# Scores-times-v as pairs of 64-row matmuls, in long one-mode stretches: a fused attention and mixer kernel

## The chip, the cores and the metric

The kernel runs on one core of a Trainium2 chip. The time is the device time of one execution in microseconds (us); where several executions are given, their median and their range are named. "The profile" is the record of one execution: a page of summaries, and a trace that can be asked for groups of instructions, waits, the chain of work that ended last, and a timeline. PE is TensorE's matmuls and PEld its weight loads, DVE is VectorE, ACT is ScalarE, POOL is GpSimd, SP is the engine that issues most transfers.

## The reference, cut to what matters

Eight batches of a gated attention without softmax, followed by an MLP mixer over tokens and then over channels:

```
B, S, D = 8, 3008, 256;  d_qk = 64;  d_tok = 256;  d_ch = 1536
scores = (z @ z.T) / S                      # S x S, symmetric
attn   = max(scores, 0) ** 2
x      = u * (attn @ v)                     # gate
h      = max(x.T @ w_tok1, 0) @ w_tok2      # over tokens
y      = x + h.T
out    = y + max(y @ w_ch1, 0) @ w_ch2      # over channels
```

All matmuls take bf16 operands and accumulate in float32.

## The kernel before, in words

**Tiles.** A batch has NQ = 6 query blocks of 512 columns (the last has 448) and NG = 6 key groups of GK = 4 tiles of 128 keys; the 24th tile of keys has 64 rows. Everything is held transposed: channels on partitions, tokens along the free axis.

**Attention, step by step.** `score_run` (L386) makes scores: one unit is two 64-row matmuls (d_qk = 64, one on the upper and one on the lower half of the array, L405) that write the two banks of one PSUM tile `sc`. `relu` evacuates a unit on ACT (L443; L431 for blocks on the diagonal) into half of an `at` tile in SBUF, and `square` squares it on DVE (L451, L479). As scores are symmetric, from batch 1 on only blocks with g >= q are computed and the others are made by a transposing DMA (`flip`, L498; `flip_tiles`, L491). `av_matmul` (L526, matmul at L539) multiplies with v: per query block, two accumulators `acc0` and `acc1` (dh = 0, 1, the two halves of the 256 channels), 23 matmuls of 128 rows each, and one of 64 rows for the last tile of keys; these two (`do_tails`, L561) run as a pair on the two halves of the array. `gate` (L622, L634) multiplies an accumulator with u on DVE into `xT`; a transposing DMA on SP makes the tile that the mixer reads.

**Mixer, in pieces.** When a batch's attention is done, `add_mixer` (L665) lists its work as pieces: 6 of `tok1` (L681, 8 matmuls of 256 columns each), 6 of `tok2` (L698), and, block by block, six of `ch1` (L742, 4 matmuls of 512 columns, evacuated as `h2pre` on ACT at L755 or on DVE at L757) and four of `ch2` (L784, 12 matmuls of 256 columns; a residual add on DVE at L797 and a store). So the mixer of batch b runs beside the attention of batch b + 1, and the mixer of batch 7 runs alone at the end.

**PSUM.** It has eight banks. `acc0` and `acc1` have one each; the other six are three two-bank tiles with the tag `ps`, taken in turn by scores, mixer pieces and early transposes (`RING = 3`, L297; `take_slot`, L661).

**What orders the work.** The program's order is computed when it is built: the loop at L1037 keeps a clock for every engine, knows what each piece costs (`column_time`, L337; a change between 64-row and 128-row matmuls costs 0.095 in `on_pe`, L343), and picks at each step among "scores", "av" (four matmuls of one accumulator, `do_half`, L586) and "mixer". A budget keeps the mixer's progress in step with the attention's, which makes the three kinds alternate piece by piece. ACT's and DVE's instructions are written in the order in which this plan starts them (`push`, L303; `run_engines`, L321). The chip then runs each engine's list in that order, with semaphores between engines.

The functions that the diff touches, with what calls them:

Of the kernel before, what the change touches and what calls it, by code (L numbers as in the profile page):

```python
# [13 lines left out]
P = 128  # L14
# [41 lines left out]
def kernel(  # L56
# [118 lines left out]
    def fill(n, tag="ps", bufs=3):  # L175

        wp = psum.tile([P, QW], F32, tag=tag, name="wp", bufs=bufs)
        for _ in range(n):
            nc.tensor.matmul(
                wp[:], zero[:, :P], zero[:], start=True, stop=True, skip_group_check=True)  # L180
# [117 lines left out]
    ring = [Done(0.0) for _ in range(RING)]  # L298
# [87 lines left out]
    def score_run(us, start):  # L386
        slots = sorted((d for d in ring if d.t is not None), key=lambda d: d.t)
        for unit in us:
            (b, q, g), pr = unit
            zT = zTs[b].rearrange("p t s -> p (t s)")  # L390
            W = widths[q]
            slot = slots.pop(0)
            ring.remove(slot)
            begin = max(start, slot.t, known(turned[b, q], turned[b, g]))
            cost = column_time(W)
            if triangle(b, q, g):

                cost = (column_time(QW), column_time(P))[pr]
            begin, start = on_pe(begin, "half", cost)
            sc = psum.tile([P, 2, QW], F32, tag="ps", name="sc", bufs=3)  # L400
            for r, i, c0, c1 in parts(unit):
                k = z_tile(b, r, g * GK + i) * P
                m = z_tile(b, r, q * GK) * P
                h = slice(r * d_qk, (r + 1) * d_qk)
                nc.tensor.matmul(  # L405
                    sc[:, r, c0:c1], zT[h, k:k + P], zT[h, m + c0:m + c1],
                    start=True, stop=True)
            if pr == 0:
                live["at"] += 1
                at_free.remove(min(at_free))  # L410
            busy = 0.92
            if triangle(b, q, g):
                busy = (0.87, 0.43)[pr]
            if grain(b, q, g) < GK and pr == 0:
                early[b, q, g] = [Done() for _ in range(GK)]
            done = push("act", begin + cost + 0.21, busy, busy + 0.16,
                        lambda t, unit=unit, sc=sc: relu(unit, sc, t))
            ring.append(done)
# [93 lines left out]
    class Block:  # L512
        def __init__(self, b, q):
            self.b, self.q, self.W = b, q, widths[q]
            self.todo = key_order(b, q)[1]
            self.slot = 0
            self.g = None
            self.steps, self.half = [], 0
            self.acc = [None] * DT
            self.tails = False  # L520
            self.parts = {}
# [4 lines left out]
    def av_matmul(blk, g, i, dh, stop):  # L526
        first = blk.acc[dh] is None
        if first:
            blk.acc[dh] = psum.tile([P, QW], F32, tag=f"acc{dh}", name=f"acc{dh}", bufs=1)
        rows = slice(0, P)  # L530
        if g * GK + i == KT - 1:
            rows = slice(dh * TAIL, (dh + 1) * TAIL)
        rhs = blocks[blk.b, blk.q, g][1][rows, i]
        o = blk.acc[dh][:, :blk.W]
        if len(rhs.shape) == 3:
            o = o.rearrange("p (j s) -> p j s", s=P)
        else:
            rhs = rhs[:, :blk.W]
        nc.tensor.matmul(  # L539
            o, vs[blk.b, g][rows, i, dh * P:(dh + 1) * P], rhs, start=first, stop=stop,  # L540
            skip_group_check=True)
# [9 lines left out]
    def block_ready(blk, g):  # L551
        e = blocks.get((blk.b, blk.q, g))
        return FAR if e is None else known(e[0])

# [6 lines left out]
    def do_tails(blk, start):  # L561
        on_pe(start, "half", column_time(blk.W))
        blk.parts.setdefault(LAST, 2)
        for dh in range(DT):
            av_matmul(blk, LAST, GK - 1, dh, False)
        blk.tails = True
        finished(blk, LAST)

    def next_half(t):

        blk = cur[0]
        if blk is None:
            return FAR, None
        if blk.g is not None:
            dh, tiles = blk.steps[blk.half]
            events = early.get((blk.b, blk.q, blk.g), [])[tiles[0]:tiles[-1] + 1]
            return max(t, known(acc_free[dh], *events)), blk.g
        at = max(t, known(acc_free[0]))
        ready = [(block_ready(blk, g), i) for i, g in enumerate(blk.todo)]
        soon = [i for r, i in ready if r <= at + 0.05]  # L580
        if soon:
            return at, blk.todo[soon[0]]
        r, i = min(ready)
        return max(at, r), blk.todo[i]

    def do_half(start, g):  # L586
# [17 lines left out]
        for i in tiles:  # L604
            av_matmul(blk, g, i, dh, final and i == tiles[-1])
        if final:
            acc_free[dh] = push(
                "dve", end + 0.21, 0.61, 0.75, lambda t, dh=dh: gate(blk, dh, t), first=1,
                room=("xT", "x") if dh == 0 else lambda: (blk.b, blk.q) in xTs)
        blk.half += 1  # L610
        if blk.half == len(blk.steps):
            blk.g = None
            finished(blk, g)
            if final:
                if blk.q == NQ - 1:
                    add_mixer(blk.b)
                m = blk.b * NQ + blk.q + 1
                cur[0] = Block(m // NQ, m % NQ) if m < B * NQ else None
# [3 lines left out]
    def gate(blk, dh, t):  # L622
        b, q, W = blk.b, blk.q, blk.W
        acc = blk.acc[dh]
# [36 lines left out]
    def take_slot():  # L661
        slot = min((d for d in ring if d.t is not None), key=lambda d: d.t)
        ring.remove(slot)

    def add_mixer(b):  # L665
# [6 lines left out]
        def tok1(q, end):  # L672
            if q == 0:
                take_slot()
                st["a_ps"] = psum.tile([P, DT, d_tok], F32, tag="ps", name="a_ps", bufs=3)
# [9 lines left out]
            if q == NQ - 1:  # L685
                def evacuate(t):
                    st["a"] = sb.tile([P, 2, D], BF16, tag="a", name="a_sb", bufs=1)
                    nc.scalar.activation(st["a"][:], st["a_ps"][:], ACT.Relu)
                    a_done.t = t
                ring.append(push("act", end + 0.21, 0.5, 0.65, evacuate, first=1))  # L690

        def tok2(q, end):
            take_slot()
            W = widths[q]
            h = psum.tile([P, DT, QW], F32, tag="ps", name="h_ps", bufs=3)
# [21 lines left out]
            ring.append(push("dve", end + 0.21, 1.12, 1.25, add))  # L717
# [12 lines left out]
        def ch1(q, c2, end):  # L730
            take_slot()
# [6 lines left out]
            hp = psum.tile([P, 2, QW], F32, tag="ps", name="hp", bufs=3)  # L738
# [12 lines left out]
            def evacuate(t):  # L751
# [6 lines left out]
                if q == NQ - 1:  # L758
                    if c2 == 0 and b % 2 == 0:
# [5 lines left out]
            ring.append(push(engine, end + 0.21, busy, busy + 0.16, evacuate,  # L765
                             done=h2_done[q, c2]))
# [3 lines left out]
        def ch2(q, half, i, end):  # L770
            apart = alone(q, half)
            if i == 0 or apart:
                take_slot()
                st["op"] = psum.tile([P, 2, D], F32, tag="ps", name="op", bufs=3)
# [18 lines left out]
            def residual(t):  # L793
# [25 lines left out]
                if over:  # L819
                    live["us"] -= 1  # L820
            ring.append(push("dve", max(end + 0.21, known(st["turned", q])), 0.62, 0.75,
                             residual))
# [44 lines left out]
    def next_piece(t):  # L867

        best = FAR, None
        slots = [d.t for d in ring if d.t is not None]  # L870
# [87 lines left out]
    def late_z(c, landed):  # L958
# [4 lines left out]
        def turn(end):  # L963
            take_slot()
            zp = psum.tile([P, GK, P], F32, tag="ps", name="zp", bufs=3)
            turn_on_pe(zr[0], zp)
            turned[0, c] = Done()
            ring.append(push(
                "dve", end + 0.2, 0.66, 0.8,
                lambda t: nc.vector.tensor_copy(zTs[0][:, c * GK:c * GK + GK, :], zp[:]),  # L970
                first=1, done=turned[0, c]))
# [5 lines left out]
    def first_u(landed):  # L977
# [3 lines left out]
        def turn(end):  # L981
            take_slot()
            up = psum.tile([P, QW // P * DT, P], F32, tag="ps", name="up", bufs=3)
# [5 lines left out]
            ring.append(push("dve", end + 0.2, 1.15, 1.3, lambda t: evacuate(up)))  # L989

        def evacuate(up):
            uTs[0, 0] = sb.tile([P, QW // P, DT, P], BF16, tag="uT", name="uT", bufs=3)
            nc.vector.tensor_copy(
                uTs[0, 0].rearrange("p t h s -> p (t h) s"), up[:])
# [19 lines left out]
    flat = NQ * NG * 1.73 + NQ * (NQ + 1) / 2 * 0.63  # L1014
    fill(7)

    for c in range(DT):
        zp = psum.tile([P, GK, P], F32, tag=f"acc{c}", name=f"zp{c}", bufs=1)
        turn_on_pe(double_first_z(c), zp)
        nc.scalar.copy(zTs[0][:, c * GK:c * GK + GK, :], zp[:])  # L1020
    for c in range(DT, GK):
        turn_first_z(c)
    fill(1)
# [12 lines left out]
    STARVED = 0.7  # L1036
    while cur[0] is not None or heads or tails:  # L1037
# [10 lines left out]
        n = can_score(done_units, RING)  # L1048
        slots = sorted(d.t for d in ring if d.t is not None)
        n_now = min(n, len(slots))  # L1050
        ts = FAR
        if n_now:
            at = max(t, has_turned(units[done_units:done_units + n_now]))
            ts = max([at] + [slots[i] - 0.1 - 0.216 * i for i in range(n_now)])
# [13 lines left out]

        pick = None

        together = (
            blk is not None and blk.q > 1 and blk.b < B - 1 and not blk.tails
            and blk.slot == 0 and t + 0.3 < tails_ready(blk) < FAR)
        if n_now and not together and ts <= t + NOW and (whole or (low and n_now >= 2)):
# [10 lines left out]
        elif budget > 0 and tm <= t + NOW:  # L1085
            pick = "mixer"
        elif ta <= t + NOW:
            pick = "av"
        elif tm <= t + NOW and (budget > -5.0 or blk is None):
            pick = "mixer"  # L1090
        else:
            options = [(ta, "av"), (tm, "mixer")]
            if n_now and (whole or low):
# [7 lines left out]
            if blk is not None and blk.b == 0 and blk.q == 0 and blk.acc[1] is None:  # L1101
                idle = int((when - t) / 0.22)
                if idle:
                    fill(idle, "acc1", 1)
            pick = what

        if pick == "scores":
            if blk is not None and tails_ready(blk) <= t + 0.3:
# [46 lines left out]
```

## Time and profile before

| what | value |
|---|---|
| median of 3 executions | 1183.68 us |
| the three executions | 1168.08, 1183.68, 1184.21 us |
| profiled execution, span from first to last instruction | 1166.2 us |
| nearest executed time to that span | 1168.08 us, 1.9 us more |
| busy: PE, DVE, ACT, POOL | 1152.4, 554.7, 509.0, 129.0 us |
| matmuls and weight loads of the program, each | 7057 |
| first weight load of batch 1's scores-times-v | at 91.84 us |
| last scores-times-v matmuls | up to 1071 us |
| last matmul starts | 1161.6 us |

The page gives no time of its own for the profiled execution besides the span. A row of the groups names the line, the engine, the operation, output and input tiles, shapes and count; then the total busy time and the mean of one in ns, and how long that engine had stood idle before these instructions, with what ended the idleness. Durations of matmuls include their way through the array, and successive ones overlap, so what a matmul costs is the distance between successive starts. A line of the timeline merges neighbours of one kind: its start, how long the group lasted up to the end of its last member, and the count. A few matmul records are missing in the trace, so counts in merged lines can be short; weight loads are complete.

### The profile page before, as it was taken

Reading aid. Unit: us, or ns where it says so; the run is one execution under the profiler, and the core shown is the slowest. Engines: PE = TensorE matmul, PEld = TensorE weight load, DVE = VectorE, ACT = ScalarE, POOL = GpSimd, SP = SyncE. Lnnn points to the kernel's source line nnn. Section 1 sums busy time; section 2 is a strip of 40 time slices with the busy share of each in tenths; the row PEclk is TensorE's granted clock in tenths of the full one; section 3 lists DMA queues with packets and bytes.
Section 4 is the critical chain, followed back from the end, with each engine's and each line's share of the span. In section 5 each row is a group of like instructions: output and inputs, shape, how many; then the busy total and the mean of one; then the engine's idle time right before and its main releaser. Section 6 shows DMA issues by size and latency. Waiting matters only on the chain.

```text
span 1166.2 us, 17678 instructions
## 1 busy us (share of the span) xinstructions
PE 1152.4 (99%) x6964; PEld 629.8 (54%) x7057; DVE 554.7 (48%) x842; ACT 509.0 (44%) x636; POOL 129.0 (11%) x281
## 2 busy tenths in 40 slices
PE   9999999999999999999999999999999999999998
PEld 3334554655546555565555645566454655555666
DVE  6666541556434563435424365243752546512544
ACT  7886552436332453344623355343442444513221
POOL 4510110102001020010300102001020001000000
PEclk9999999999999999999999999999999999999999
DMA  8999596987969789895979859686897968442121
GB/s 161 185 178 193 125 159 135 163 152 137 168 127 172 148 144 164 116 184 126 117 178 160 174 119 174 153 162 115 169 158 138 176 132 169 92 101 55 50 82 64
DMA packets 472500, 165.54 MB, mean 142 GB/s; under 512 B 436256, under 2 KB 450144, under 8 KB 472416
## 3 DMA queue, kind: packets, MB, share of 16 engines
q1 hardware_dynamic: 444560, 131.70, 57.2%
q0 software_dynamic: 27344, 32.32, 20.9%
q8 instruction: 55, 0.90, 0.3%
q10 hardware_dynamic: 512, 0.38, 0.1%
q14 instruction: 29, 0.24, 0.1%
HBM read 65.40 MB, written 24.64 MB: 77 GB/s over the span
## 4 chain that ended last, share of the span: by engine, by line
PE 96%; DMA 2%; issue 1%; DVE 1%; POOL 0%; ACT 0%; SPq 0%; DVEq 0%
PE acc L539 41%; PE op L784 21%; PE hp L742 21%; PE sc L405 7%; PE a_ps L681 4%; PE h_ps L698 3%; DMA v_sb<-in_v_dram 1%; DMA zf<-in_z_dram 0%; DVE xT L707 0%; POOL v_sb L190 0%; DVE h2pre L757 0%; DVE at L479 0%; ACT at L443 0%; SPq L156 0%; ACT at L431 0%
## 5 line engine op out<-in xcount | busy, mean ns | idle before, releaser
L443 ACT ACTIVATE at<-sc 128x1024 bf16<-128x1024 f32 (+1 forms) x284 | 271.5, 1022 | 220.8 <-PE sc L405 219.8
L539 PEld LDWEIGHTS <-v_sb 128*128 128x128 bf16 (+1 forms) x2304 | 209.3, 97 | 269.9 <-issue 65.6
L539 PE MATMUL acc<-at,v_sb 128*128 128x512 bf16 (+3 forms) x1443 | 347.9, 378 | 3.1 <-DMA v_sb<-in_v_dram 1.1
L755 ACT ACTIVATE h2pre<-hp 128x1024 bf16<-128x1024 f32 (+1 forms) x177 | 177.7, 1006 | 314.1 <-PE hp L742 311.4
L451 DVE TENSOR_TENSOR at<-at 128x1024 bf16<-128x1024 bf16 (+1 forms) x284 | 194.9, 689 | 186.1 <-ACT at L443 185.7
L742 PE MATMUL hp<-xT,w_ch_sb 128*128 128x512 bf16 (+1 forms) x1113 | 261.9, 374 | 2.5 <-DVE xT L707 0.4
L784 PE MATMUL op<-w_ch_sb,h2pre 128*128 128x256 bf16 x2208 | 258.1, 273 | 0.1
L784 PEld LDWEIGHTS <-h2pre 128*128 128x128 bf16 x2208 | 215.9, 98 | 46.0 <-DVE h2pre L757 0.4
L539 PE MATMUL acc<-fl,v_sb 128*128 128x512 bf16 (+1 forms) x817 | 193.1, 370 | 1.4 <-issue 0.5
L742 PEld LDWEIGHTS <-w_ch_sb 128*128 128x128 bf16 x1152 | 112.7, 98 | 126.6 <-issue 0.9
L757 DVE TENSOR_SCALAR h2pre<-hp 128x1024 bf16<-128x1024 f32 (+1 forms) x111 | 133.7, 1204 | 58.9 <-PE hp L742 58.8
L797 DVE TENSOR_TENSOR res<-op,u_sb 128x512 f32<-128x512 f32 x87 | 60.2, 692 | 194.9 <-PE op L784 193.5
L634 DVE TENSOR_TENSOR xT<-acc,uT 128x512 bf16<-128x512 f32 (+1 forms) x96 | 63.5, 666 | 121.1 <-PE acc L539 120.7
L405 PE MATMUL sc<-zT 64*128 64x512 bf16 (+1 forms) x732 | 94.6, 360 | 0.5 <-ACT zT L1020 0.2
L431 ACT ACTIVATE at<-sc 128x512 bf16<-128x512 f32 (+3 forms) x164 | 59.1, 449 | 60.0 <-PE sc L405 59.6
L190 POOL DMA_DIRECT2D v_sb<-in_v_dram x48 | 26.0, 545 | 413.7 <-PE acc L539 398.3
L405 PEld LDWEIGHTS <-zT 64*128 64x128 bf16 x732 | 31.2, 94 | 54.8 <-issue 36.3
L479 DVE TENSOR_TENSOR at<-at 128x512 bf16<-128x512 bf16 (+3 forms) x164 | 43.7, 320 | 29.4 <-ACT at L431 29.2
L707 DVE TENSOR_TENSOR xT<-xT,h_ps 128x1024 bf16<-128x1024 bf16 (+1 forms) x48 | 54.2, 1170 | 0.7 <-PE h_ps L698 0.6
L698 PE MATMUL h_ps<-w_tok_sb,a_sb 128*128 128x512 bf16 (+1 forms) x182 | 43.8, 374 | 0.6
L681 PE MATMUL a_ps<-x_sb,w_tok_sb 128*128 128x256 bf16 x384 | 44.0, 273 | 0.0
L681 PEld LDWEIGHTS <-w_tok_sb 128*128 128x128 bf16 x384 | 37.6, 98 | 6.5
(46 smaller groups left out, 170.4 us busy)
## 6 DMA issues: line engine op xcount, KB each, us to landing
out_dram<-res SPq DMA_DIRECT2D x87, 256.0 KB, 2.4
v_sb<-in_v_dram POOLq DMA_DIRECT2D x40, 256.0 KB, 5.8
ur<-in_u_dram POOLq DMA_DIRECT2D x40, 256.0 KB, 5.7
w_tok_sb<-in_moe_w_tok_dram POOLq DMA_DIRECT2D x10, 256.0 KB, 9.1
zs<-in_z_dram POOLq DMA_DIRECT2D x35, 64.0 KB, 4.7
at<-at SPq DMA_TRANSPOSE x123, 2.4
fl<-at SPq DMA_TRANSPOSE x105, 4.0
v_sb<-in_v_dram POOLq DMA_DIRECT2D x8, 192.0 KB, 9.1
```

Source lines behind the costliest of these rows:

```text
L405: nc.tensor.matmul(sc[:, r, c0:c1], zT[h, k:k + P], zT[h, m + c0:m + c1], start=True, stop=True)
L443: nc.scalar.activation(view, sv, ACT.Relu, scale=inv_S)
L451: nc.vector.tensor_mul(view, view, view)
L539: nc.tensor.matmul(o, vs[blk.b, g][rows, i, dh * P:(dh + 1) * P], rhs, start=first, stop=stop, skip_group_check=True)
L634: nc.vector.tensor_mul(xT[:, dh, :full * P].rearrange("p (t s) -> p t s", s=P), acc[:, :full * P].rearrange("p (t s) -> p t s", s=P), uT[: ...
L681: nc.tensor.matmul(st["a_ps"][:, th, :], w_tok1_sb[:, k, th * P:(th + 1) * P], x[:, :, i, :], start=(k == 0 and th == 0), stop=(k == KT - ...
L698: nc.tensor.matmul(h[:, dh, :W], st["a"][:, th, dh * P:(dh + 1) * P], w_tok2_sb[:, th, q * QW:q * QW + W], start=(th == 0), stop=(th == 1))
L742: nc.tensor.matmul(hp[:, r, :W], w_ch1_sb[:, dc, cc * P:(cc + 1) * P], xT[:, dc, :W], start=(dc == 0), stop=(dc == DT - 1))
L755: nc.scalar.activation(h2[:, :, :W], hp[:, :, :W], ACT.Relu)
L757: nc.vector.tensor_single_scalar(h2[:, :, :W], hp[:, :, :W], 0.0, AX.max)
L784: nc.tensor.matmul(op[:, i, :], h2, w_ch2_sb[:, cc, :], start=(cc == 0 and (i == 0 or apart)), stop=(cc == CHT - 1), skip_group_check=True)
L797: nc.vector.tensor_add(res.rearrange("p i (h d) -> p i h d", d=P), op.rearrange("p i (h d) -> p i h d", d=P), us[:, :, half * 2:half * 2 + ...
```

## The change

1. From batch 1 on, each 128-row matmul of scores-times-v is written as two 64-row matmuls, on the upper and the lower half of the array, that accumulate in the two banks of one two-bank tile. Batch 0 keeps the old form (renamed `whole_matmul`, `do_whole`, `next_whole`).
2. The accumulators lose their own two banks. All eight banks are now four two-bank slots (`bank_pair`). The fourth holds batch 0's two accumulators (`first_acc`), and joins the ring afterwards; from batch 1 on `acc0` and `acc1` take a slot each from the ring for the length of a block.
3. At the end of a block, `finish` sums the two banks: a copy of the second bank on ACT into a float32 tile `cp` (from the `res` buffers), an add of the first bank on DVE, and then the gate from `cp` instead of from PSUM. The slot is free after the add.
4. The picking rule from batch 1 on goes by mode: after 128-row work it stays with the mixer as long as a piece can run and the budget is above -2; after 64-row work it stays with scores (one unit at a time) and scores-times-v, and goes to the mixer only between blocks with a positive budget, or if nothing else can run.

```diff
+    def bank_pair(slot, name):
+        return psum.tile([P, 2, QW], F32, tag=f"ps{slot}", name=name, bufs=1)
+    ROWS = [slice(0, P // 2), slice(P // 2, P)]
...
-    ring = [Done(0.0) for _ in range(RING)]
+    ring = [(Done(0.0), i) for i in range(RING)]
+    first_acc = bank_pair(RING, "first_acc")
...
-            sc = psum.tile([P, 2, QW], F32, tag="ps", name="sc", bufs=3)
+            sc = bank_pair(slot, "sc")
...
+    def av_matmul(blk, g, i, dh, h, stop):
+        rows = ROWS[h]
+        rhs = blocks[blk.b, blk.q, g][1][rows, i]
+        o = blk.acc[dh][:, h, :blk.W]
...
+        nc.tensor.matmul(
+            o, vs[blk.b, g][rows, i, dh * P:(dh + 1) * P], rhs,
+            start=(dh, h) not in blk.begun, stop=stop, skip_group_check=True)
...
+    def do_half(start, g):
+        blk = cur[0]
+        if blk.whole:
+            return do_whole(start, g)
...
+            blk.steps = [(dh, tiles) for dh in range(DT)]
+            if g == LAST:
+                blk.steps.insert(0 if blk.slot > 1 else DT, (None, [GK - 1]))
+        dh, tiles = blk.steps[blk.half]
+        final = blk.slot == NG and dh is not None
+        if dh is not None and blk.acc[dh] is None:
+            blk.home[dh], free_at = take_slot()
+            blk.acc[dh] = bank_pair(blk.home[dh], f"acc{dh}")
+            start = max(start, free_at)
+        start, end = on_pe(start, "half", len(tiles) * column_time(blk.W))
+        for i in tiles:
+            for h in range(2):
+                av_matmul(blk, g, i, h if dh is None else dh, h, final and i == tiles[-1])
+        if final:
+            finish(blk, dh, end)
...
+    def finish(blk, dh, end):
+        W, acc = blk.W, blk.acc[dh]
+        summed = Done()
+        ring.append((summed, blk.home[dh]))
+        def copy(t):
+            cp = sb.tile([P, QW], F32, tag="res", name="cp", bufs=3)
+            nc.scalar.copy(cp[:, :W], acc[:, 1, :W])
+            push("dve", t, 0.66, 0.78, lambda t: add(cp, t), first=1, done=summed)
+        def add(cp, t):
+            nc.vector.tensor_add(cp[:, :W], acc[:, 0, :W], cp[:, :W])
+            push("dve", t, 0.58, 0.7, lambda t: gate(blk, dh, cp, t), first=1,
+                 room=("xT", "x") if dh == 0 else lambda: (blk.b, blk.q) in xTs)
+        push("act", end + 0.21, 0.46, 0.61, copy, first=1)
...
-    flat = NQ * NG * 1.73 + NQ * (NQ + 1) / 2 * 0.63
+    flat = NQ * NG * 1.73 + NQ * (NQ + 1) / 2 * 0.44
...
+    BACKLOG = 0.9
+    SWING = 2.0
...
-        n = can_score(done_units, RING)
+        runs = blk is not None and blk.whole
+        most = RING if runs else 1
+        n = can_score(done_units, most)
...
+        spare = True
+        if blk is not None and not runs:
+            if None in blk.acc:
+                spare = len(slots) > 1 and slots[1] <= t + NOW
+            elif blk.slot == NG and blk.g is None:
+                spare = len(slots) > 1
+            elif blk.slot == NG and blk.half == len(blk.steps) - 1:
+                spare = len(slots) > 1 and slots[1] <= t + 0.8
+        between = blk is None or blk.acc[0] is None
+        mixer_now = tm <= t + NOW and (budget > -SWING or blk is None)
...
+        if not runs:
+            if mode[0] == "full" and mixer_now:
+                pick = "mixer"
+            elif mode[0] == "half" and between and budget > 0 and mixer_now:
+                pick = "mixer"
+            elif n_now and spare and queued < BACKLOG and ts <= t + NOW:
+                pick = "scores"
+            elif ta <= t + NOW:
+                pick = "av"
+            elif n_now and spare and ts <= t + NOW:
+                pick = "scores"
+            elif mixer_now:
+                pick = "mixer"
```

## The prediction

> **What bounds the kernel now.** I read the page from the top: busy shares, the slices with PE's clock, then the chain that ended last.
>
> ```profile
> span 1166.2 us, 17678 instructions
> PE 1152.4 (99%) x6964; PEld 629.8 (54%) x7057; DVE 554.7 (48%) x842; ACT 509.0 (44%) x636; POOL 129.0 (11%) x281
> PEclk9999999999999999999999999999999999999999
> PE 96%; DMA 2%; issue 1%; DVE 1%; POOL 0%; ACT 0%; SPq 0%; DVEq 0%
> ```
>
> PE is on the path for 96% of the span at an undiminished clock; DVE and ACT work less than half of it. So the kernel ends when PE has gone through its list, and a change counts by what it does to PE's list or to PE's waits. A busy share of 99% does not say that PE streams all the time, because a matmul's recorded time includes its way through the array. So next comes the timeline of PE in a stretch where scores and scores-times-v alternate, and one line of ACT's:
>
> ```profile
> 544.66 1.46 PE L539 MATMUL acc<-fl,v_sb 128*128 128x512 bf16 x6
> 546.05 0.39 PE L539 MATMUL acc<-at,v_sb 64*128 64x512 bf16 x2
> 546.28 0.81 PE L405 MATMUL sc<-zT 64*128 64x512 bf16 x6
> 547.02 2.33 PE L539 MATMUL acc<-at,v_sb 128*128 128x512 bf16 x10
> 549.28 0.71 PE L405 MATMUL sc<-zT 64*128 64x256 bf16 x6
> ```
>
> ```profile
> 505.93 2.86 ACT L443 ACTIVATE at<-sc 128x1024 bf16<-128x1024 f32 x3 [3.29 <-PE sc L405]
> ```
>
> Ten full matmuls go from 547.02 to 549.28: 2.26 us, of which 10 x 0.216 = 2.16. What is left is 0.10: the change from 128-row to 64-row mode. Likewise 544.66 to 546.05 is 1.39 = 6 x 0.216 + 0.094, and the six score matmuls, three pairs, take 546.28 to 547.02 = 0.74 = 3 x 0.216 + 0.092. From this view I take three prices. A 512-column matmul costs 0.216. A pair of 64-row matmuls costs the same 0.216 as one full one. A change of mode costs 0.096, in either direction (the single starts in the trace agree: 0.312 from a full start to the first 64-row start, against 0.216). One finer point: the first pair after a change takes 0.225 (546.05 to 546.28 is 0.23).
>
> With these I checked the whole. The weight loads of the trace, which name their rows, change between 64 and 128 rows 272 times: 59 before batch 1 starts at 91.84, 213 after. From 91.84 to the last matmul's start at 1161.6 are 1069.8 us. The matmuls of that stretch by count and width: scores-times-v 7 x 46 x (5 x 0.216 + 0.189) = 408.6, scores and 64-row tails 63.8, mixer 572.3, together 1044.7. The 213 changes x 0.096 add 20.4. That leaves 4.7 of true waiting. So 20 us is all that mode changes can give, and there is hardly any other slack.
>
> **What the Trainium skill says.** "TensorEngine Tiling (Array Packing)", Key Properties: changing the tiling mode drains TensorE. The trace agrees and gives the price, 0.096. The same page, Gotcha 1: different row tiles write different PSUM banks and cannot use the same one at the same time. That is why each half gets its own bank and a sum at the end is needed; in the trace a score pair writes two banks too. "TensorE: Matmul & The Clock Gate", Part 3, What overlaps and what doesn't: a weight load is pulled ahead of running matmuls where its row group differs or it goes to the background buffer, so pairs should hide their loads. The trace shows it for runs of up to four pairs, at 0.216 apiece; no longer run exists here. The tiling page's PSUM Bottleneck section warns that tiling does not speed up evacuation; here this means two added instructions per accumulator.
>
> **The change part by part.**
>
> *Mode changes.* In the changed program's order of PE instructions, 64-row and 128-row stretches alternate: 46 of each from the first new pair to the end, 91 changes. The median 64-row stretch is 11.0 us (94 matmuls of scores-times-v, up to 24 of scores), the last 128-row one 83 us. 213 - 91 = 122 changes fewer: 122 x 0.096 = -11.7. Also 60 fewer first pairs (106 - 46) x 0.009 = -0.5.
>
> *Matmuls.* Batches 1 to 7 have 7 x 6 x 46 = 1932 full matmuls that become pairs; PE's list grows by 1932 matmuls and 1932 weight loads. Streaming stays 0.216 per pair, so 0. Bounds: four instructions per 0.216 us must be issued; the chain of waits shows ch2 doing "1127.44 5.24 PE op L784 x48", 0.109 per load and matmul, the same rate over 48. For the 448-column blocks (7 x 46 = 322 pairs) the few 448-column score pairs start 0.189 to 0.194 apart: 0 to +1.6, I take +0.8. A gain isn't possible, since the columns are the same.
>
> *The sum of two banks.* 42 blocks x 2: a copy on ACT (nearest row L431 and L688, 512 columns: 0.597), an add on DVE (nearest L797: 0.692); the gate (L634: 0.666) stays, now from SBUF. ACT gains 84 x 0.597 = 50, and 16 h2pre evacuations move from it to DVE (161 for 177 in the order): -16. DVE gains 84 x 0.692 + 16 x 1.204 = 77. ACT goes to some 543, DVE to some 632, both below 55% of the span: PE covers them, cost 0. If the cover were gone, one finish costs 0.21 + 0.60 + 0.05 + 0.69 + 0.05 = 1.6 before its slot is free. Behind the copy on ACT stand relus and h2pre evacuations, behind the add on DVE squares and residuals; PE waits for those through its slots. SP's turn of xT starts about 1.3 later per block; tok1 that needs it comes a stretch later. The order of SP's 519 and POOL's 285 instructions keeps its kinds and counts, so no transfer is added.
>
> *Slots.* In before six banks served scores and mixer; now accumulators hold two of four slots for a block, leaving two. From the changed order I summed PE's work between the last matmul of a slot's user and the first of the next. After an accumulator (84 cases): 2.0 at least, median 4.4, 27 under 2.8. After a score unit (290 cases): median 1.94, only two of 1.08 under 1.48. A score needs 0.21 + 1.02 + 0.05 = 1.3; ACT takes 0.92 per unit when they follow each other (the line above: (2.86 - 1.02) / 2), and PE offers one unit per 1.08 (four pairs and a unit). After ch2: 13 of 94 cases between 1.23 and 1.39 against 0.21 + 0.69 + 0.05 = 0.95. So unqueued everything but the two fits, and queueing decides. Bounds: 0 if no engine is late; 27 x 0.8 = +22 if each short accumulator handover finds a whole relu (1.02) and a whole evacuation (1.2) ahead of it (1.6 + 2.2 = 3.8, against some 2.6 to 3.0 offered). I take +2: the order puts the finishing copy first as soon as it is ready, and other engines are half empty.
>
> *Attention operands.* With scores made in stretches, is `at` in time? From a block's last score matmul to its first use in the changed order PE has at least 3.7 us for direct blocks (needed: 1.3 + 0.7), 19.5 for flipped ones (needed in addition: 4.0 to landing, by the page's transfers), 13.6 on the diagonal. Cost 0; only in batch 1 is it below 6. Batch 0's order is the same matmul by matmul.
>
> *Sum.* -11.7 - 0.5 + 0.8 + 2.0 = -9.4. The waiting of 4.7 and the 4.6 after the last matmul stay. Span 1166.2 - 9.4 = 1156.8. The lowest executed time, 1168.08, is 1.9 above the span, so an execution like the profiled one would take 1158.7. The median of the runs shown is 15.6 higher; nothing in the profile says why, so I carry that offset: 1183.68 - 9.4 = 1174.3, 0.8% less.
>
> **The rivals.**
>
> *A, as summed (0.60).* 1174.3, own range 1170 to 1180: from -13 (no new waits, no loss in narrow pairs, part of the 4.7 gone) to -4.
>
> *B, waits at slots eat it (0.18).* Place: the 27 short accumulator handovers and the 189 score handovers under 2.0. For: only two slots rotate beside the accumulators, and ACT has a stretch with 10 units and two copies, 10 x 0.92 + 2 x 0.54 = 10.3 of 12.1 us. Against: the median accumulator handover leaves 4.4 for 1.6. At 0.45 per short accumulator handover, 12 us in place of 2: +0.6, so 1184.
>
> *C, pairs do not keep 0.216 in long runs (0.12), slower.* Place: each of the 1932 pairs. One mechanism: both weight loads (0.094 each, 0.188 if one waits for the other) plus their hand-over no longer hide behind the running pair once nothing is preloaded. For: no run of before is longer than four pairs, and the first pair after a change does take 0.009 more. Against: the third and fourth pairs are at 0.216. Each 0.010 costs 19.3. No change is reached at +5 ns, 2% slower (+23.7) at +17 ns per pair: (9.4 + 23.7) / 1932. At 0.236: +38.6 - 9.4 = +29, 1213.
>
> *D, faster by over 2% (0.10).* The whole 20.4 of mode changes is not enough for 23.7. It comes only if the changed kernel's executions lie about 1158.7 and the median shown stays: 2.1% below it.
>
> That the change doesn't do what it says is not open: the order shows 91 changes for 213.
>
> **How the numbers follow.** The likeliest is A: 1174.3. The range reaches from 1156 (D in) to 1192 (B in), leaving out C and a remainder, some 0.15. About 2% is what a measurement of this kernel can tell from no change, as the three runs lie 1.4% apart. Over 2% faster: D, 0.10. Within 2%: A and B, 0.78. Slower: C, 0.12.
>
> **What would show it.** PE's 64-row stretches of some 11 us, with scores-times-v pairs starting 0.216 apart (C wrong) or more (C right). PE busy and clock as before, PE still over 94% of the chain. Copies near 0.6 and adds near 0.7 on ACT and DVE. Waits of PE for ACT or DVE in the list of waits in all near 5 to 8 us; 15 or more would be B. Span 1157. I would be wrong if a mode change is not a fixed 0.096 but partly a wait that long stretches keep, or if ACT lags whole stretches behind.

## The result, and the profile after

The changed kernel takes 1226.32 us in the median of 4 executions (1224.08 to 1227.79); against the kernel before the ratio is 1.0444, with a 95% interval of 1.0361 to 1.0527. It is slower by over 4%, where the forecast was 0.8% faster. The executions of the kernel before lie in two groups, near 1168 and near 1183, and the ratios count both; beside the later experiments its median is 1168.9 to 1169.4, so the 15.6 that the prediction carried as an offset belongs to the three executions that it had.

The page of the changed kernel, the lines that answer to those shown of before:

```profile
span 1226.0 us, 21807 instructions
PE 1159.9 (95%) x8989; PEld 649.9 (53%) x8989; DVE 631.5 (52%) x942; ACT 548.0 (45%) x704; POOL 130.3 (11%) x281
PEclk9999999979999699999999979999999999999999
PE 87%; DMA 10%; DVE 1%; ACT 1%; issue 0%; SPq 0%; ACTq 0%; POOL 0%
```

DVE and ACT grew to what the working said (632 and 543). PE is down from 96% to 87% of the chain that ended last, and DMA is up from 2% to 10%. The clock row has dips at three places. PE's timeline in a stretch of 64-row work, in the same columns as before:

```profile
606.74 0.38 PE L409 MATMUL sc<-zT 64*128 64x512 bf16 x2
606.96 1.03 PE L629 MATMUL acc<-at,v_sb 64*128 64x512 bf16 x8
607.82 0.38 PE L409 MATMUL sc<-zT 64*128 64x512 bf16 x2
608.04 1.03 PE L629 MATMUL acc<-at,v_sb 64*128 64x512 bf16 x8
608.90 0.38 PE L409 MATMUL sc<-zT 64*128 64x512 bf16 x2
```

A score pair and four pairs of scores-times-v take 606.74 to 607.82 = 1.08 = 5 x 0.216, again and again. So pairs keep their pace in long runs. The list of waits on PE shows what doesn't keep it:

```profile
PE sc L409 <- ACT at L447: 42.3, 5, 19.9
PE a_ps L780 <- ACT at L447: 8.3, 4, 3.7
PE acc L629 <- DMA at<-at: 3.3, 2, 2.9
```

Score matmuls wait 42 us for relus, in five waits of which one has 19.9. And in ACT's own list of waits the relu stands because of a transfer:

```profile
ACT at L447 <- DMA fl<-at: 63.3, 11, 21.1
```

`fl<-at` is the flip, the transposing DMA that reads an `at` tile. The relu writes into an `at` tile: it waits until the flip that still reads that buffer has landed. The chain of the changed kernel between 236 and 270 us shows one such case:

```profile
236.62 0.79 PE hp L842 x4
237.41 21.42 DMA fl<-at
...
258.94 1.03 ACT at L447
...
260.01 0.61 PE sc L409 x2
260.62 1.71 PE acc L629 x8
```

A flip takes 21.42 us, where the median landing is 4.0 on the page of before and 4.1 on this one. PE stands from 244.8 to 260.0. After that eight matmuls take 1.71 in place of 0.86: the Trainium skill says in "TensorE: Matmul & The Clock Gate", What's actually happening, that PE's clock is halved after an idle window (the page's 3.4 us) and restored only after a busy one; the trace agrees, with a granted clock of 0.50 from 250 to 260, 0.53 from 260 to 265 and 1.00 from then on. What shares the transfer engines with that flip is on POOL's timeline, first of before, then of the changed kernel, both at the end of batch 1's attention:

```profile
206.60 0.56 POOL L190 DMA_DIRECT2D v_sb<-in_v_dram  x1 [53.35 <-PE acc L539]
209.17 0.53 POOL L190 DMA_DIRECT2D v_sb<-in_v_dram  x1 [2.00 <-PE acc L539]
...
224.01 0.53 POOL L201 DMA_DIRECT2D ur<-in_u_dram  x1 [0.20 <-issue]
224.64 0.53 POOL L190 DMA_DIRECT2D v_sb<-in_v_dram  x1
...
227.78 0.53 POOL L190 DMA_DIRECT2D v_sb<-in_v_dram  x1 [2.31 <-PE acc L539]
```

```profile
227.60 0.57 POOL L195 DMA_DIRECT2D v_sb<-in_v_dram  x1 [6.65 <-PE sc L409]
...
229.55 0.53 POOL L195 DMA_DIRECT2D v_sb<-in_v_dram  x1 [1.07 <-PE sc L409]
230.07 0.54 POOL L206 DMA_DIRECT2D ur<-in_u_dram  x1
231.30 0.53 POOL L195 DMA_DIRECT2D v_sb<-in_v_dram  x1 [0.69 <-PE sc L409]
233.24 0.53 POOL L195 DMA_DIRECT2D v_sb<-in_v_dram  x1 [1.42 <-PE sc L409]
```

In both kernels the next batch's v tiles have eight buffers of which the present batch uses six; the last four loads wait until the last query block has used a tile for the last time. Before, that block was spread between mixer pieces, so the four loads came over 21 us. Now it is one stretch of 11 us, and they come within 5.6 (one load of u lies between them in both kernels), just when that stretch's flips are issued. SP's lines for the flips, of before and then of the changed kernel:

```profile
227.43 1.69 SPq L498 DMA_TRANSPOSE fl<-at  x1
```

```profile
229.37 21.60 SPq L502 DMA_TRANSPOSE fl<-at  x2
```

Issuing two flips holds SP's list for 21.60 us, where one took 1.69 before; the transposes behind them in the list start only after that. The changed kernel's transfers in windows (last column GB/s, the one before it the share of the DMA engines' time, which counts the whole length of every transfer that starts in the window and so can exceed 1):

```profile
215.00:230.00 15.00, 15.00 (x122) 9.37 (x122) 8.44 (x11) 7.32 (x9) 2.32 (x6) 1.00 0.34 85
230.00:245.00 15.00, 14.77 (x136) 6.86 (x131) 8.57 (x18) 11.09 (x16) 3.59 (x9) 1.00 1.31 77
```

From 230 to 245 the transfer engines are busy throughout and move 77 GB/s. A gap here is the part of the distance between two successive matmul starts that the prices of the matmul and of a mode change don't account for. Over the whole trace, the 10 gaps of over 1 us add up to 55.1 us: 15.4 and 20.1 at the ends of batches 1 and 2, smaller ones about the later ends, and 3.1 inside batch 1.

### The profile page after: what moved, and what is told of

Read it like the earlier page. It is cut to its first block, busy times and chain, and to the rows that moved or that the text cites. A ratio compares the mean times of both kernels' runs of the same rounds, so it can differ in the third digit from the quotient of the medians.

```text
span 1226.0 us, 21807 instructions
## 1 busy us (share of the span) xinstructions
PE 1159.9 (95%) x8989; PEld 649.9 (53%) x8989; DVE 631.5 (52%) x942; ACT 548.0 (45%) x704; POOL 130.3 (11%) x281
## 4 chain that ended last, share of the span: by engine, by line
PE 87%; DMA 10%; DVE 1%; ACT 1%; issue 0%; SPq 0%; ACTq 0%; POOL 0%
PE acc L629 30%; PE op L885 20%; PE hp L842 19%; DMA fl<-at 9%; PE sc L409 5%; PE first_acc L546 5%; PE a_ps L780 4%; PE h_ps L798 3%; ACT at L447 1%; DVE xT L731 1%; DMA zf<-in_z_dram 1%; DMA v_sb<-in_v_dram 0%; DMA at<-at 0%; DVE xT L807 0%; DVE h2pre L857 0%
## 5 line engine op out<-in xcount | busy, mean ns | idle before, releaser
L629 PEld LDWEIGHTS <-v_sb 64*128 64x128 bf16 x3948 | 199.4, 95 | 222.5 <-issue 18.7
L629 PE MATMUL acc<-at,v_sb 64*128 64x512 bf16 x2268 | 286.1, 382 | 3.3 <-DMA at<-at 3.3
L855 ACT ACTIVATE h2pre<-hp 128x1024 bf16<-128x1024 f32 (+1 forms) x161 | 159.8, 1003 | 288.2 <-PE hp L842 287.9
L629 PE MATMUL acc<-fl,v_sb 64*128 64x512 bf16 (+1 forms) x1680 | 193.7, 367 | 1.0 <-DVE xT L807 0.7
L857 DVE TENSOR_SCALAR h2pre<-hp 128x1024 bf16<-128x1024 f32 (+1 forms) x127 | 153.1, 1205 | 70.2 <-PE hp L842 69.5
L409 PE MATMUL sc<-zT 64*128 64x512 bf16 (+1 forms) x732 | 124.6, 365 | 42.4 <-ACT at L447 42.3
L712 DVE TENSOR_TENSOR cp<-acc,cp 128x512 f32<-128x512 f32 (+1 forms) x84 | 56.6, 676 | 128.1 <-ACT cp L708 126.6
L708 ACT COPY cp<-acc 128x512 f32<-128x512 f32 (+1 forms) x84 | 48.8, 581 | 133.5 <-PE acc L629 133.4
L546 PE MATMUL first_acc<-at,v_sb 128*128 128x512 bf16 (+2 forms) x288 | 65.5, 376 | 3.9 <-DVE xT L731 3.2
L731 DVE TENSOR_TENSOR xT<-cp,uT 128x512 bf16<-128x512 f32 (+1 forms) x84 | 55.2, 665 | 3.6 <-PE hp L842 2.3
```

Source lines behind the costliest of these rows:

```text
L409: nc.tensor.matmul(sc[:, r, c0:c1], zT[h, k:k + P], zT[h, m + c0:m + c1], start=True, stop=True)
L546: nc.tensor.matmul(o, vs[blk.b, g][rows, i, dh * P:(dh + 1) * P], rhs, start=first, stop=stop, skip_group_check=True)
L629: nc.tensor.matmul(o, vs[blk.b, g][rows, i, dh * P:(dh + 1) * P], rhs, start=(dh, h) not in blk.begun, stop=stop, skip_group_check=True)
L731: nc.vector.tensor_mul(xT[:, dh, :full * P].rearrange("p (t s) -> p t s", s=P), acc[:, :full * P].rearrange("p (t s) -> p t s", s=P), uT[: ...
L855: nc.scalar.activation(h2[:, :, :W], hp[:, :, :W], ACT.Relu)
L857: nc.vector.tensor_single_scalar(h2[:, :, :W], hp[:, :, :W], 0.0, AX.max)
```

## Experiments

The theory: the loads of v and u are not slower as such, but they now fall into the few microseconds in which flips are made; flips beside loads land late, their `at` buffers come free late, ACT's relus stand, and PE with a list of fixed order stands behind them (**collision**). Rivals: one stretch's flips are too many by themselves (**burst**); PE waits for late data, not for buffers (**late data**).

**e1: no v loads after batch 1.**

```diff
     def load_v(b, c):
+        if b > 1:
+            vs[b, c] = vs[1, c]
+            loading(LOAD)
+            return
```

> The changed kernel, but v is loaded for batches 0 and 1 only; later batches multiply with batch 1's v, so that part of the result is of other data. Nothing else in the order of instructions changes. Theory 1 (collision): the next batch's v loads wait for their buffers until the last block's 10 us stretch frees them all, then run beside the flips of that stretch, which land 20 us late, and PE stands at scores whose at buffer is not free. Then the gaps of over 8 us are gone: 1160 to 1175 us. Theory 2 (burst): the flips of one stretch are by themselves too many for the transfers, v has no part: over 1210 us, with gaps of 15 and 20 us at the same places.

1166.06 us; ratio to before 0.9958 (0.9932 to 0.9983). The gaps of 15 and 20 us are gone; one of 4.8 at the end of batch 2 stays. The flips' number and places in the order are those of the changed kernel, so the burst theory is out: flips alone don't do it.

**e2, e3, e4: a control, more `at` buffers, v loads spread.** All three keep only the first 512 columns of w_tok2, for room.

```diff
 e3:
-            ats[b, q, g] = sb.tile([P, GK * QW], BF16, tag="at", name="at", bufs=ROOM["at"])
+            ats[b, q, g] = sb.tile([P, GK * QW], BF16, tag="at", name="at", bufs=ROOM["at"] + 2)
 e4:
-            vt = sb.tile([P, GK, D], BF16, tag="v", name="v_sb", bufs=8)
+            vt = sb.tile([P, GK, D], BF16, tag="v", name="v_sb", bufs=12)
...
-                    at_group(base + (NQ - 1) * NG - 2 + (j if j > 1 else 0),
+                    at_group(base + 8 + 4 * j,
                              lambda b=b, c=c: load_v(b + 1, c))
```

> A control for the next two: the changed kernel with only the first 512 columns of w_tok2 kept in SBUF and used for all blocks (that part of the result is of other weights), which frees 10 KB a partition and drops five loads in batch 0. Both theories: as the changed kernel, 1226 us, within 5.

> The control with eight at buffers in place of six; the order of all engines stays (the plan still counts six), so only the wait of relu for a free at buffer is relaxed by two blocks. Theory 1 and 2 both, if the wait is one for a free buffer: gaps at scores shrink by most of their 48 us, 1165 to 1185 us. Theory 3 (late data): PE would wait for the late flips' data anyway, the wait moves to scores-times-v: over 1205 us.

> The control with twelve v buffers in place of eight, and the loads of the next batch's v asked for one by one, four steps apart, from the second block on, so that the same bytes are loaded but not in one stretch. Theory 1: 1160 to 1178 us. Theory 2: over 1210 us.

The control: 1227.58, ratio 1.0453 (1.0366 to 1.0540), as the changed kernel. With eight `at` buffers: 1193.36, ratio 1.0166 (1.0086 to 1.0247), 34 us better than the control and 8 above the range that I gave. Two more buffers take away most of the waits of scores for relus (16.8 us in two waits, from 48.8 in four), while 8.4 us of waits for transferred data remain (v 4.9, and 3.5 for `at<-at`, the transposes within diagonal blocks; the control has 5.5 for the latter alone). So it is mainly the buffers' release that PE waited for, and late data is a small part. With v's loads spread: 1170.87, ratio 0.9988 (0.9963 to 1.0013). The same bytes, with four more buffers and at other moments, cost 57 us less. The largest gap left, 7.3 us, is in batch 1; why it is there wasn't tried.

**e5, e6, e7: a version with nothing left out, the pairs undone in it, and before without v.**

```diff
 e5:
-        x = sb.tile([P, DT, QW // P, P], BF16, tag="x", name="x_sb", bufs=ROOM["x"])
+        x = sb.tile([P, DT, QW // P, P], BF16, tag="x", name="x_sb", bufs=6)
...
-        ur = sb.tile([P, QW // P, D], BF16, tag="ur", name="ur", bufs=3)
+        ur = sb.tile([P, QW // P, D], BF16, tag="ur", name="ur", bufs=2)
...
-            vt = sb.tile([P, GK, D], BF16, tag="v", name="v_sb", bufs=8)
+            vt = sb.tile([P, GK, D], BF16, tag="v", name="v_sb", bufs=10)
...
-                    at_group(base + (NQ - 1) * NG - 2 + (j if j > 1 else 0),
+                    at_group(base + (10 + 5 * j if j < 4 else (NQ - 1) * NG - 2 + j),
 e6, on e5:
+        tail = g * GK + i == KT - 1
+        if h and not tail:
+            return
+        rows = ROWS[h] if tail else slice(0, P)
...
-        o = blk.acc[dh][:, h, :blk.W]
+        o = blk.acc[dh][:, 0, :blk.W]
...
-            nc.scalar.copy(cp[:, :W], acc[:, 1, :W])
+            nc.scalar.copy(cp[:, :W], acc[:, 0, :W])
 e7, on the kernel before:
     def load_v(b, c):
+        if b > 1:
+            vs[b, c] = vs[1, c]
+            loading(LOAD)
+            return
```

> The changed kernel with nothing left out: ten v buffers in place of eight, paid for by one buffer less for the mixer's x tiles and one less for u's, and four of the next batch's six v loads asked for early, five steps apart; the last two stay in the last block. Theory 1 (the v loads' burst beside the flips): most of the 55 us of gaps go, 1160 to 1175 us, at or under the kernel before. Theory 2: over 1210 us.

> e5 with the same order, but each pair of 64-row matmuls of scores-times-v is one 128-row matmul into the first bank; copy and add both read that bank, so the output is twice the product. 565 changes of mode in place of 91. If a change costs a fixed 0.096 us: e5 plus 474 x 0.096 = 45 us. If part of the 0.096 is a wait that is hidden in denser alternation: less than 35.

> The kernel before, with v loaded for batches 0 and 1 only (later batches use batch 1's v). If the v loads are hidden there: 1164 to 1170 us, no change. If they cost the kernel before as well, and e1's gain was in part that: under 1160.

e5: 1182.54, ratio 1.0101 (1.0055 to 1.0146); 44 us of the loss are back, but I expected more: its profiled execution has 23.6 us in gaps of over 1 us, the two large ones in batch 1 (9.5 and 5.0). e6: 1222.26, 40 us over e5. The profiled spans are 1220.6 and 1187.7; less their gaps (9.3 and 23.6) they are 47 apart, which is 474 changes of 0.100. After its gaps e5 also has more matmuls at half the clock; an estimate of that from the granted clock (7.8 us in e5, 3.7 in e6) gives 0.108 in place of 0.100. In e6's own trace a 512-column start is followed by the first 64-row start after 0.312, as in before. So no part of the price is hidden in denser alternation. e7: 1168.42, ratio 1.0002 (0.9975 to 1.0028): the kernel before hid v's loads entirely, so e1's gain is none of before's.

**e8 and e9: loads at the ends of blocks.** Nothing is left out.

```diff
 e8, on e5:
-                    at_group(base + (10 + 5 * j if j < 4 else (NQ - 1) * NG - 2 + j),
+                    at_group(base + (35 if j > 3 else 23 if b == 1 else 11 + 6 * j),
 e9, on e8:
-                at_group(base + q * NG + 2, lambda m=m: load_u(m // NQ, m % NQ))
-                at_group(base + q * NG + 5, lambda m=m: turn_u(m // NQ, m % NQ))
+                ask = base + q * NG + (5 if b else 2)
+                at_group(ask + (6 if b else 3), lambda m=m: turn_u(m // NQ, m % NQ))
+                at_group(ask, lambda m=m: load_u(m // NQ, m % NQ))
```

> e5 with its early v loads moved to the last step of a block, so that they run while PE is in the mixer and no flips are being made: four at the end of batch 1's fourth block, which a 41 us mixer stretch follows, later one at the end of each block; the last two at the end of the last block. Nothing left out. Theory 1: the gaps left in e5 (9.5 and 5.0 us in batch 1, 24 in all) fall below 10 us: 1160 to 1172 us, under the kernel before. If any load of the same bytes costs the same, wherever it is: 1178 to 1186 as e5.

> e8 with u's loads of batches 1 to 7 moved to the last step of a block too, and u's turn one block later. Theory 1, if u's loads in a stretch slow the flips as v's do: 3 to 8 us under e8, 1155 to 1167 us. If u's single loads are harmless: as e8 within 3 us.

e8: 1180.39, ratio 1.0061 (1.0028 to 1.0095), not told apart from e5, outside my range and inside that of the alternative, by which the same bytes cost the same wherever they are loaded. But its waits have moved: in its profiled execution no score matmul waits for a relu any more, and 6.7 us at `tok1` for relus and 4.7 for transposes of diagonal blocks are left. e9: 1164.71, ratio 0.9934 (0.9904 to 0.9964): 16 us under e8, twice what I expected, and faster than both kernels, though by 0.7% only over before; its 22 executions lie between 1158.35 and 1174.92. The same bytes do not cost the same everywhere, then, and I had put too little on u: its six loads a batch, each in the middle of a stretch, were left as the partners that flips met. The page of e9:

```profile
span 1156.6 us, 21836 instructions
PEclk9999999999999999999999999999999999999999
PE 97%; DVE 1%; DMA 1%; ACT 0%; issue 0%; SPq 0%; POOL 0%
```

Here PE, once started, never waits for over 1 us, the clock has no dip, and PE is back at 97% of the chain. The list of waits on PE no longer has any for a relu's `at`. The longest landing of a flip is 14.0 us, where the changed kernel has 27.4 and before 17.8. A window of e9 over the end of the same batch, with its stretch of 64-row work:

```profile
229.00:244.00 15.00, 15.00 (x134) 6.82 (x132) 8.95 (x18) 12.79 (x18) 1.93 (x5) 1.00 1.14 191
```

The transfer engines are about as busy as in the window of the changed kernel above (1.14 for 1.31), but they move 191 GB/s in place of 77. Two loads of u and v are in flight at some time in this window, six in that one. e9 doesn't keep flips and loads apart altogether: 50 of its 105 flips have a load of u, v or z in flight beside them, against 37 in the changed kernel. But only 6 have four loads or more, against 19.

**e10 and e11: u's loads alone, and the loads of e9 in the kernel before.** e10 has only e9's edit of u's loads and of u's turn (the transpose of a loaded u tile, on SP), on the changed kernel; e11 has the edits of e5, e8 and e9 to buffers and loads, on the kernel before.

> The changed kernel with only u's loads moved to the last step of a block (buffers and v's loads as in the change). Theory 1 with v as its main part: the gaps of 15 and 20 us stay in good part, 1195 to 1220 us. If u's loads in the stretches are the main part: under 1185.

> The kernel before with all that e9 does to loads and buffers (ten v buffers, v's and u's loads at block ends), its matmuls and picking rule untouched. If the loads cost it nothing: 1165 to 1171 us, so that e9's gain over before is the change's own. If e9 gains by its loads alone: about 1160, as e9.

e10: 1204.57, ratio 1.0258 (1.0206 to 1.0311); the large gaps halve to 8.4 and 8.9. That is within the range for v as the main part. So moving u's loads, with u's turn, gives back 22 us, v's alone (with the buffers, e8) 46, both 62. Two things in this are not separated. With u's loads the turn of u, a transpose on SP, came a block later too: in the changed kernel SP's list stood before that turn, waiting for u's load, for 9.9 us at 557 and 9.2 at 702, with flips behind it, and in e10 it no longer does after batch 0. And ten v buffers with v's loads asked for at the old places were not run. e11: 1186.54, ratio 1.0148 (1.0123 to 1.0172), slower than before, which neither answer had: a wait of scores for relus of 9.4 us appears at 102 us, and one of scores for a residual add (L797) of 3.8 at 868. A likely reason is that no mixer stretch follows the end of a block there. So e9's gain isn't one that the loads bring by themselves. Which of e11's loads causes its waits wasn't tried.

## Why the prediction was wrong

*What bounds the kernel, and the prices, held.* A pair at 0.216 in runs of 94 matmuls, a mode change at 0.096 to 0.108, 150 changes in the trace's weight loads (59 before batch 1, 91 after) are as worked out. The sum gave a span of 1156.8. e9, which differs from the change in its loads, u's turn and three buffer counts alone, has 1156.6. The sum is one for an execution without long waits: 1156.6 is the fastest execution of e9, as 1166.2 is one of the fastest of before, and in medians e9 is 4.6 us under before (1164.71 against 1169.33), half of the 9.4. That the two spans agree to 0.2 is partly luck, as 2.8 of the sum were picked between bounds, for slots and narrow pairs. D did not come either: the fastest execution of e9 is 0.8% under the fastest of before beside it (1158.35 and 1167.94).

*The sum of two banks held.* Copies take 0.581 and adds 0.676, and neither engine holds PE up in e9.

*Slots (rival B) were not it.* The 42 us of waits look like B, scores that wait for ACT, and pass its mark of 15. The slots did come late, but not for B's reason of too few slots and a queue on ACT: ACT stood idle with a full slot in front of it, because the `at` buffer behind was not free. B's place and price were wrong.

*C fell.* Pairs didn't slow down.

*The step that failed is "Attention operands", and with it "no transfer is added" under the sum of two banks.* Three things were wrong in it. It asked when an `at` tile's data is first needed (at least 3.7, 13.6 or 19.5 us after its last score matmul, by the kind of block), put the cost at 0, and never asked when its buffer has to be free again for the next relu; the wait that came was that one: 63.3 us of ACT on flips, and behind it 42.3 of PE's scores on ACT. It took the median landing of 4.0 for every flip, where the page gives only a median; the longest in before's own trace is 17.8. In that trace 73 flips have no load of u, v or z in flight beside them and land within 5.6 us; 32 have one, and nine of these take over 10. The changed kernel has 68 within 5.6 and 37 with loads, nine of them over 10, up to 27.4. (A slow flip also meets more loads, so the counts alone don't tell cause from effect; e1 and e4 do.) So slow flips were there before, but no engine waited for one.

Third, the prediction counted transfers by kind, found none added and priced SP's and POOL's queues at nothing. When the attention's order was squeezed from some 23 us per block (979 us for 42 blocks) to stretches of 11 us, the releases that start the v loads were squeezed with it, and so were the flips. The Trainium skill has the shared resource in "Trainium Kernel Development and Optimization", Key Constraints: transfers issued from SP, ACT and POOL run on the same 16 DMA engines and interleave. The trace agrees (a flip at 21.42 beside five loads), and the prediction should have followed it up.

*The account.* 1226.0 - 1156.6 = 69.4 us between the changed kernel and e9. Gaps of over 1 us are 55.1 of it (none in e9), gaps between 0.25 and 1 us are 1.7 (8.7 against 7.0). The remaining 12.6 fit the matmuls that start after a gap at half the clock, such as the first eight at 1.71 for 0.86: an estimate from the granted clock (28.7 us of PE's work right after gaps, at 0.51 to 0.60 of the clock) is 13.6. That share was not isolated by a run.

What stays open is why transposing transfers and plain loads slow each other so far, to 77 GB/s. The runs show that they do, and that having fewer loads in flight while flips are made takes the waits away; the mechanism inside the transfer engines wasn't tried.

## What to carry to other kernels

When a change reorders the engine that bounds a kernel, ask of each buffer not only when its data is needed, but when it is given back, and which transfers its release starts: a stretch that is twice as dense starts them twice as densely. For a transfer take the spread of its landing times as well as the median, and look at what hides the slow ones now. If transposing transfers and loads share the DMA engines, spread the loads, and put as few as possible where transposes are made in a row.

## What the runs showed of the hardware

Pairs of 64-row matmuls into two banks run at the pace of one 128-row matmul for a whole block (the chain of the changed kernel has 94 in 10.15 us, 0.216 per pair), so in this kernel a row split cost PE nothing; its price is the sum at the end. A change between the two forms cost 0.096 to 0.108 us. With six loads in flight beside flips the transfers moved 77 GB/s in 15 us, with two 191, at shares of the DMA engines' time of 1.31 and 1.14. Flips without a load of u, v or z beside them landed within 5.6 us in both kernels and within 6.1 in e9; the slowest beside loads took 27.4. A wait of 15 us cost more than its length, because PE then ran at a granted clock of 0.53 for 5 us.
